# The first pair's scores as one float32 product of 66 rows

## The chip, the cores and the metric

The kernel runs on one core of a Trainium2 chip. The metric is the device time of one execution, in microseconds (us); lower is better. Each version's time is a median of several executions. A profiled execution has a time of its own; its span runs from the first to the last recorded instruction of the core.

In the rows, PE is TensorE's matmuls and PEld its weight loads, DVE is VectorE, ACT is ScalarE, POOL is GpSimd, and SP is the queue from which all this kernel's DMAs are issued, in order.

## The reference, cut to what matters

A causal attention with a decay bias feeds two feed-forward blocks. There are 4 batches of 8 heads, 576 positions and head size 64; the model width is 512.

```python
# attention, per head
scores = (q @ k.T) / sqrt(64)
cum    = cumsum(max(s, 0))
bias   = -(cum[q] - cum[k])                 # one number a position
scores = where(causal, -1e9, scores + min(bias, 0))
attn   = softmax(scores);  out = attn @ v
# block 1: gelu(x @ w_in) -> u, v; layer norm of v; u * (w_sg @ v_n + b_sg); x + (...) @ w_out
# block 2: mixes x with its shifted self by mu_k, mu_r; relu(xk @ w_k)**2 @ w_v * sigmoid(xr @ w_r)
```

## The kernel before, in words

Heads go through `attn_pair` in pairs, 16 pairs in all: pair 0 holds heads 0 and 1, pair 1 heads 2 and 3, and so on. The first four pairs, those of batch 0, come before any feed-forward work; later pairs are interleaved with `moe1`. While pairs 0 to 3 run, a generator called `prologue` converts the weights of block 1 from their 64-bit words: seven conversions (`sraw0` to `sraw6`). Conversion 0 to 3 fill `wv`, 4 to 6 fill `wcs`.

**Scores before.** A product of full accuracy is made of two fast ones. For each head the kernel loads keys and queries into one tile `kq` (keys in rows 0 to 63, queries in rows 64 to 127). ACT, DVE or POOL then cast them to the fast type fp32r (`qb`, `ka`), the rest that the cast loses is taken by two subtractions (`split_lo`), two DMAs copy the casts to the other half of the partitions (`qa`, `ka`), and two more put the running sums `cum`, split in the same way into `crt`, into rows of `QB` and `KB`. Each score chunk is then two matmuls of 128 rows: L252 with `qa`, `ka` and L253 with `qb`, `kb`.

**What follows a score chunk.** DVE adds the mask, takes the row minimum and writes `st` (L277). ACT takes the exponential (L285). PE transposes (`tp`), ACT or DVE copies the transposes to `pt`, and PE multiplies with the values (`pv`, L338, plain float32). Score chunks take turns in two PSUM banks, so PE may be at most two chunks ahead of DVE. A pair has nine steps: four of its first head, one that holds the last 64 rows of both heads, four of its second head. Its score chunks are of 128, 256, 384 and 512 columns for each head, and 512, 512, 64 and 64 for the common step: 3,712 columns.

**Buffers.** `kq` has two buffers, so a head's load has to wait until the casts and subtractions of the head two places earlier are done. A weight conversion takes three instructions on ACT (L76, L81, L87) and three on DVE (L82, L84, L69).

**What sets the order.** Each engine and the SP queue execute strictly in order. The order is set by a scheduler when the program is built; `PRO` says after how much of the attention each step of `prologue` is offered to it, and `after(late, early)` puts one instruction behind another in that order, without a wait. At most eight DMAs are in flight: DMA number i waits for number i - 8.

Of the kernel before, what the change touches and what calls it, by code (L numbers as in the profile page):

```python
# [8 lines left out]
F32 = mybir.dt.float32  # L9
# [28 lines left out]
def fused_kernel(ctx, tc, kqT, vL, s, w_in, g_ln, w_sgT, b_sg, w_out, mu_k, mu_r, w_k, w_v, w_r, out):  # L38
# [18 lines left out]
    def constants():  # L57
        after(nc.sync.dma_start(out=g_sb, in_=g_ln), last_row[0])
        nc.sync.dma_start(out=bsg, in_=b_sg.partition_broadcast(P))
        nc.sync.dma_start(out=mu[:, 0, 0], in_=mu_k)  # L60
        nc.sync.dma_start(out=mu[:, 1, 0], in_=mu_r)
        nc.vector.tensor_scalar(out=mu[:, :, 1], in0=mu[:, :, 0], scalar1=-1.0, scalar2=1.0, op0=ALU.mult, op1=ALU.add)
# [44 lines left out]
    qaf, kaf = (ep.tile([P, S], F32R, tag="u", name=n, bufs=4) for n in ("qa_f", "ka_f"))  # L107
    sums = [at.tile([P, 9], F32, tag=f"sums{i}", name=f"sums{i}", bufs=1) for i in range(2)]
# [7 lines left out]
    with tc.high_priority():  # L116
# [16 lines left out]
    make_identity(nc, ident)  # L133
    nc.gpsimd.memset(mhalf, -0.5)
    nc.gpsimd.memset(mask, 0.0)
    nc.gpsimd.affine_select(
        out=mask[:, 512:], in_=mask[:, 512:], pattern=[[-1, P]], compare_op=ALU.is_ge,
        fill=-BIG, base=0, channel_multiplier=1,
    )
# [65 lines left out]
    last_row = [None]  # L205


    def attn_pair(b, hp):
# [3 lines left out]
        for hh in range(2):  # L212
            h = 2 * hp + hh
            hd = b * H + h

            kq = at.tile([P, S], F32, tag="kq", name=f"kq{hd}", bufs=2)
# [645 lines left out]
```

## Time and profile before

| | |
|---|---|
| median of 3 executions | 679.77 us (679.13 to 683.0) |
| the profiled execution | 679.44 us |
| its span | 677.7 us; 1.74 us lie outside it |
| PE busy | 645.2 us, 95% of the span |
| DVE, ACT, POOL busy | 479.1, 416.0 and 219.7 us |
| DMA | 112.74 MB, mean 166 GB/s |

The busy shares are means over stages with different limits. The profile's 40 slices of 16.9 us show PE below 90% busy in its first five slices (3, 8, 6, 9, 9 tenths) and again around the eighth; from there on it is full to the end. [...]

### The profile page before, as it was taken

Reading aid. Unit: us, or ns where it says so; the run is one execution under the profiler, and the core shown is the slowest. Engines: PE = TensorE matmul, PEld = TensorE weight load, DVE = VectorE, ACT = ScalarE, POOL = GpSimd, SP = SyncE. Lnnn points to the kernel's source line nnn. Section 1 sums busy time; section 2 is a strip of 40 time slices with the busy share of each in tenths; the row PEclk is TensorE's granted clock in tenths of the full one; section 3 lists DMA queues with packets and bytes.
Section 4 is the critical chain, followed back from the end, with each engine's and each line's share of the span. In section 5 each row is a group of like instructions: output and inputs, shape, how many; then the busy total and the mean of one; then the engine's idle time right before and its main releaser. Section 6 shows DMA issues by size and latency. Waiting matters only on the chain.

```text
span 677.7 us, 11532 instructions
## 1 busy us (share of the span) xinstructions
PE 645.2 (95%) x3912; PEld 553.5 (82%) x3912; DVE 479.1 (71%) x995; ACT 416.0 (61%) x940; POOL 219.7 (32%) x233
## 2 busy tenths in 40 slices
PE   3869999799999999999999999999999999999997
PEld 2547676779878988877988899988888988999997
DVE  7876679986668645469644388787875959677863
ACT  5878777785558656368653285587755779543530
POOL 8556646368436459237363030000000000000000
PEclk9969999999999999999999999999999999999999
DMA  7764652455453532733510675567744593546643
GB/s 227 221 205 140 186 167 73 138 158 158 152 186 102 143 115 55 240 117 90 163 37 15 214 268 183 164 224 222 255 164 163 188 361 136 168 182 195 225 139 117
DMA packets 56459, 112.74 MB, mean 166 GB/s; under 512 B 7680, under 2 KB 20624, under 8 KB 56400
## 3 DMA queue, kind: packets, MB, share of 16 engines
q1 hardware_dynamic: 56400, 112.01, 52.3%
q8 instruction: 31, 0.51, 0.3%
q14 instruction: 28, 0.23, 0.1%
HBM read 74.46 MB, written 28.02 MB: 151 GB/s over the span
## 4 chain that ended last, share of the span: by engine, by line
PE 83%; DVE 6%; DMA 6%; ACT 2%; SPq 1%; issue 1%; POOL 0%; DVEq 0%; ACTq 0%; POOLq 0%
PE k L368 15%; PE sg L368 9%; PE pv L338 8%; PE r L368 7%; PE o L368 7%; PE psa L771 7%; PE u L368 6%; PE v L368 5%; PE tp L303 5%; PE psb L771 4%; PE sc L252 4%; PE sc L253 3%; PE psc L771 2%; DMA kq<-in_kqT_dram 1%; DMA wc<-wscr 1%
## 5 line engine op out<-in xcount | busy, mean ns | idle before, releaser
L368 PE MATMUL k<-x,wk 128*128 128x512 f32 (+1 forms) x480 | 101.4, 372 | 0.0
L368 PEld LDWEIGHTS k<-x,wk 128*128 128x128 f32 x480 | 83.6, 188 | 17.4
L252 PE MATMUL sc<-ka,qa 128*128 128x512 f32 (+3 forms) x180 | 64.0, 366 | 21.6 <-DVE mx L277 10.8
L285 ACT ACTIVATE st<-st,mx 128x128 f32<-128x128 f32 (+4 forms) x124 | 72.0, 582 | 19.3 <-DVE mx L277 18.8
L277 DVE CUSTOM_DVE_ANT_0 st<-sc,mask 128x512 f32<-128x512 f32 (+3 forms) x124 | 61.1, 503 | 27.7 <-PE sc L253 24.4
L368 PE MATMUL sg<-wsg,vn 128*128 128x288 f32 x448 | 65.2, 298 | 0.9 <-DVE u L502 0.9
L338 PE MATMUL pv<-pt,vf 128*64 128x320 f32 (+4 forms) x448 | 64.8, 366 | 0.2 <-ACT pt L305 0.2
L368 PEld LDWEIGHTS sg<-wsg,vn 128*128 128x128 f32 x448 | 60.8, 188 | 1.5 <-DVE u L502 1.1
L252 PEld LDWEIGHTS sc<-ka,qa 128*128 128x128 f32 x180 | 33.9, 189 | 32.1 <-DVE mx L277 15.1
L253 PE MATMUL sc<-KB,QB 128*128 128x512 f32 (+3 forms) x180 | 57.4, 335 | 1.0 <-DVE wv L69 1.0
L338 PEld LDWEIGHTS pv<-pt,vf 128*64 128x64 f32 x448 | 35.5, 137 | 23.5 <-issue 5.2
L303 PE MATMUL tp<-ident,st 128*128 128x128 f32 x300 | 49.5, 282 | 1.2 <-ACT st L285 1.0
L368 PE MATMUL r<-x,wr 128*128 128x512 f32 (+1 forms) x240 | 50.6, 372 | 0.0
L368 PEld LDWEIGHTS r<-x,wr 128*128 128x128 f32 x240 | 41.7, 188 | 8.8
L368 PE MATMUL v<-wv,xs 128*128 128x512 f32 x192 | 48.5, 397 | 0.0
L69 POOL TENSOR_TENSOR qa<-kq,QB 64x576 fp32r<-64x576 f32 x29 | 45.1, 1555 | 3.1 <-POOL st_f L283 1.0
L229 POOL CAST QB<-kq 64x576 fp32r<-64x576 f32 x28 | 21.1, 757 | 73.6 <-PE sc L253 44.3
L69 POOL TENSOR_TENSOR KB<-kq,ka 64x576 fp32r<-64x576 f32 x29 | 43.5, 1499 | 3.9 <-ACT ka L230 1.9
L303 PEld LDWEIGHTS tp<-ident,st 128*128 128x128 f32 x300 | 35.6, 142 | 10.6 <-ACT st L285 4.6
L368 PE MATMUL o<-gh,wc 128*128 128x288 f32 x192 | 40.8, 298 | 0.8 <-DMA wc<-wscr 0.8
L368 PEld LDWEIGHTS v<-wv,xs 128*128 128x128 f32 x192 | 35.1, 188 | 7.5 <-POOL QB L229 0.5
L368 PE MATMUL u<-xs,wc 128*128 128x288 f32 x288 | 40.9, 297 | 0.0
(188 smaller groups left out, 1451.8 us busy)
## 6 DMA issues: line engine op xcount, KB each, us to landing
wc<-wscr SPq DMA_DIRECT2D x24, 512.0 KB
kq<-in_kqT_dram SPq DMA_DIRECT2D x32, 288.0 KB
kr<-kdram SPq DMA_DIRECT2D x12, 768.0 KB
kdram<-k SPq DMA_DIRECT2D x16, 512.0 KB
yt<-ydram SPq DMA_DIRECT2D x24, 257.0 KB
vf<-in_vL_dram SPq DMA_DIRECT2D x16, 320.0 KB
ydram<-y SPq DMA_DIRECT2D x16, 288.5 KB
gt<-gdram SPq DMA_DIRECT2D x12, 384.0 KB
```

Source lines behind the costliest of these rows:

```text
L69: eng.tensor_tensor(out=lo, in0=x, in1=f32(hi), op=ALU.subtract)
L229: (nc.scalar.copy if hd < 2 else nc.gpsimd.tensor_copy)(qb[64:128], kq[64:128])
L252: nc.tensor.matmul(sc[:m, :c1 - c0], qa[:, q], ka[:, c0:c1], start=True, stop=False)
L253: nc.tensor.matmul(sc[:m, :c1 - c0], qb[:, q], kb[:, c0:c1], start=False, stop=True)
L277: mi = nc.vector.tensor_tensor_reduce(out=st[:, c0:c1], in0=sc[:, :n], in1=mk, op0=ALU.add, op1=ALU.min, scale=-SCALE, scalar=mx[:, 0:1] i ...
L285: e = nc.scalar.activation(st[:, :w], st[:, :w], AF.Exp, bias=mx[:, last:last + 1], scale=-1.0, accum_out=sm[:, i + 5 * (hh == 1):i + 5 * ...
L303: nc.tensor.transpose(tp[:, c:c + P], st[:, j * P:(j + 1) * P], ident)
L338: nc.tensor.matmul(acc[64 * a:64 * a + 64, o:n], vf[:, a, kk], pt, start=(kk == 0), stop=(kk == nk - 1))
L368: nc.tensor.matmul(acc, a, w_, start=(i == 0), stop=(i == n - 1))
L771: nc.tensor.matmul(ps[:, c, :HW], l, r, start=(start and i == 0), stop=(i == len(mms) - 1), skip_group_check=True)
```

## The change

The change is in the first microseconds and in the order of the DMAs behind them. It does six things.

1. Heads 0 and 1 no longer use `kq`, the casts, the subtractions and the copies. Queries go straight into rows 0 to 63 of a float32 tile `QF`, keys into rows 0 to 63 of `KF`. Row 64 of `QF` holds `cum` and row 64 of `KF` holds -1; row 65 of `QF` holds 1 and row 65 of `KF` holds `cum`. One plain float32 matmul over these 66 rows gives score and bias together.
2. `cum` goes to those rows directly, as an unsplit float32 row, by four small DMAs.
3. The casts of heads 2 and 3 move to ACT (they stood on POOL and DVE), and those of heads 0 and 1 are gone.
4. The raw weights' first two loads are put behind those four rows (`first_rows`), and so are the values' load of pair 0; the four loads of `constants` (`g_sb`, `bsg`, two of `mu`) all stand behind the last sums issued so far, where before only the first did.
5. The sets of `QB` and `KB` are filled in another order, those of `QB` on DVE.
6. `PRO` offers the first conversion at once, the second and third after pair 0, and the others closer together.

```diff
     def constants():
-        after(nc.sync.dma_start(out=g_sb, in_=g_ln), last_row[0])
-        nc.sync.dma_start(out=bsg, in_=b_sg.partition_broadcast(P))
-        nc.sync.dma_start(out=mu[:, 0, 0], in_=mu_k)
-        nc.sync.dma_start(out=mu[:, 1, 0], in_=mu_r)
+        for i in (nc.sync.dma_start(out=g_sb, in_=g_ln),
+                  nc.sync.dma_start(out=bsg, in_=b_sg.partition_broadcast(P)),
+                  nc.sync.dma_start(out=mu[:, 0, 0], in_=mu_k),
+                  nc.sync.dma_start(out=mu[:, 1, 0], in_=mu_r)):
+            after(i, last_row[0])
...
+    QF = [ep.tile([P, S], F32, tag="xT", name=f"QF{i}", bufs=8) for i in range(2)]
+    KF = [ep.tile([P, S], F32, tag="xT", name=f"KF{i}", bufs=8) for i in range(2)]
...
-        for i in range(NSET + 1):
-            eng = nc.gpsimd if i else nc.vector
-            eng.memset(f32(QB[i][0:64]), 1.0)
-            eng.memset(f32(KB[i][0:64]), 0.0)
-            eng.memset(f32(KB[i][0:4]), -1.0)
+        for i in range(2):
+            nc.vector.memset(QF[i][64:66], 1.0)
+            nc.gpsimd.memset(KF[i][64:66], -1.0)
...
+    for i in range(NSET + 1):
+        nc.vector.memset(f32(QB[i][0:64]), 1.0)
+        nc.gpsimd.memset(f32(KB[i][0:64]), 0.0)
+        nc.gpsimd.memset(f32(KB[i][0:4]), -1.0)
...
-                if i == 0:
-
-                    after(d, last_row[0])
+                if i < 2:
+                    after(d, first_rows[0])
...
+            if pr < 1:
+                qf, kf = QF[hh], KF[hh]
+                nc.sync.dma_start(out=qf[0:64], in_=kqT[b, h][64:128])
+                nc.sync.dma_start(out=kf[0:64], in_=kqT[b, h][0:64])
+                nc.sync.dma_start(out=qf[64:65], in_=cum[hd:hd + 1])
+                last_row[0] = nc.sync.dma_start(out=kf[65:66], in_=cum[hd:hd + 1])
+                ops.append((qf, kf))
+                if hh == 0:
+                    vf, x_t, load_v = outputs(b, hp, pr, h)
+                elif hd == 1:
+                    after(load_v, last_row[0])
+                    first_rows[0] = last_row[0]
+                yield 0
+                continue
...
-            (nc.scalar.copy if hd < 2 else nc.gpsimd.tensor_copy)(qb[64:128], kq[64:128])
-            (nc.vector.tensor_copy if 1 < hd < H else nc.scalar.copy)(ka[0:64], kq[0:64])
+            (nc.scalar.copy if hd < 4 else nc.gpsimd.tensor_copy)(qb[64:128], kq[64:128])
+            (nc.vector.tensor_copy if 3 < hd < H else nc.scalar.copy)(ka[0:64], kq[0:64])
...
-            lo = nc.vector if hd == 0 else nc.gpsimd
-            split_lo(lo, qa[64:128], kq[64:128], qb[64:128])
-            split_lo(lo, kb[64:128], kq[0:64], ka[0:64])
+            split_lo(nc.gpsimd, qa[64:128], kq[64:128], qb[64:128])
+            split_lo(nc.gpsimd, kb[64:128], kq[0:64], ka[0:64])
...
         def scores(sc, hh, q, c0, c1, m):
+            if len(ops[hh]) == 2:
+                qf, kf = ops[hh]
+                nc.tensor.matmul(sc[:m, :c1 - c0], qf[0:66, q], kf[0:66, c0:c1], start=True, stop=True)
+                return
             qa, ka, qb, kb = ops[hh]
...
-    PRO = [0, 0] + [1 + 0.75 * i for i in range(5)]
+    PRO = [1e-6, 2.05, 2.05, 2.3, 2.6, 3.25, 4]
```

The first place is DVE's start. Here `scr` holds the sums (the TENSOR_SCALAR clips them, and the scan that stands as SCALAR_TENSOR_TENSOR adds them up), and `crt` their split. Before:

```order
L122 MEMSET scr_97 32x576
L126 MEMSET QB0_84 64x576
L127 MEMSET KB0_86 64x576
L129 TENSOR_SCALAR scr_97<-scr_97 32x576
L128 MEMSET KB0_86 4x576
L130 SCALAR_TENSOR_TENSOR scr_97<-scr_97 32x576
L69 TENSOR_TENSOR qa0_130<-kq0_126,QB0_84 64x576
L69 TENSOR_TENSOR KB0_86<-kq0_126,ka0_131 64x576
L69 TENSOR_TENSOR crt_98<-scr_97,crt_98 32x576
```

DVE's start in the changed kernel:

```order
L125 MEMSET scr_101 32x576
L127 MEMSET QF0_92 2x576
L127 MEMSET QF1_93 2x576
L140 MEMSET QB0_84 64x576
L140 MEMSET QB1_85 64x576
L140 MEMSET QB_f_88 64x576
L135 TENSOR_SCALAR scr_101<-scr_101 32x576
L136 SCALAR_TENSOR_TENSOR scr_101<-scr_101 32x576
L70 TENSOR_TENSOR crt_102<-scr_101,crt_102 32x576
L301 ISA st_f0_147,mx0_0_0_148<-sc0_0_0_0_149,mask_83 128x128
```

Six memsets now stand ahead of the TENSOR_SCALAR where three did, the one between it and the scan is gone, and the two subtractions of head 0 are gone too.

The second place is the SP queue where the loads of heads 4 and 5 (`kq4`, `kq5`) stand. Before, they come behind the copies of heads 3 and 4, and `kq5` behind the reciprocals of pair 0 (`rdram`):

```order
L217 DMA kq4_528<-in_kqT_dram 128x576
L222 DMA QB1_85<-crt_98 2x1x576
L223 DMA KB1_87<-crt_98 2x1x576
L232 DMA ka3_349<-ka3_349 64x576
L231 DMA qa3_348<-QB0_84 64x576
L232 DMA ka4_533<-ka4_533 64x576
L188 DMA sraw4_415<-in_w_in_dram 128x4x256 x2
L231 DMA qa4_532<-QB1_85 64x576
L321 DMA rdram_65<-rc0_298 9x128
L217 DMA kq5_543<-in_kqT_dram 128x576
```

In the changed kernel they stand behind the second raw weight (`sraw0` here names the tile that weights 0 and 1 share) and the constants, the 23rd to 33rd DMA:

```order
L163 DMA sraw0_153<-in_w_in_dram 128x1024
L160 DMA cumd_62<-crt_102 32x1152
L58 DMA g_sb_67<-in_g_ln_dram 128x4
L59 DMA bsg_68<-in_b_sg_dram 128x576
L60 DMA mu_69<-in_mu_k_dram 128x4
L61 DMA mu_69<-in_mu_r_dram 128x4
L241 DMA kq4_508<-in_kqT_dram 128x576
L246 DMA QB1_85<-crt_102 2x1x576
L247 DMA KB1_87<-crt_102 2x1x576
L241 DMA kq5_523<-in_kqT_dram 128x576
L163 DMA sraw2_329<-in_w_in_dram 128x1024 x2
```

So `kq5` has moved ahead of the third and fourth raw weight and of `rdram`, while the constants have moved back to just before `kq4`.

The third place is DVE behind pair 0's common step, in the changed kernel. `syt0` is a weight in conversion, `mu` the small instruction on the two `mu` loads, `ka4` the cast of head 4:

```order
L70 TENSOR_TENSOR wv_98<-syt0_154,wv_98 128x512
L301 ISA st_f0_147,mx0_2_4_193<-sc0_2_4_0_194,mask_83 128x512
L301 ISA mx0_2_4_193 128x1
L301 ISA st_f0_147,mx0_2_4_193<-sc0_2_4_1_198,mask2_131,mx0_2_4_193 128x64
L301 ISA mx0_2_4_193 128x1
L63 TENSOR_SCALAR mu_69<-mu_69 128x2x4
L83 SCALAR_TENSOR_TENSOR syt0_154<-sraw0_153,syt0_154 128x512
L301 ISA st0_1_0_214,mx0_1_0_215<-sc0_1_0_0_216,mask_83 128x128
L301 ISA mx0_1_0_215 128x1
L254 CAST ka4_513<-kq4_508 64x576
```

Before, the instruction on `mu` stood ahead of DVE's first score chunk, both of these conversions were through before the second head's first chunk, and no cast of head 4 stood here.

## Rows read from the trace of the kernel before

**Rows 1.** Busy time in four stretches (us, then busy us and count per engine, PEclk).

```profile
12.65:45.99 33.34, 24.58 (x125) 17.52 (x125) 26.60 (x65) 26.27 (x69) 18.11 (x16) 0.87 0.64 187
...
45.99:78.60 32.61, 31.17 (x211) 21.94 (x211) 20.78 (x65) 28.73 (x82) 23.25 (x20) 0.98 0.58 173
...
37.35:47.59 10.24, 8.07 (x30) 6.22 (x32) 9.06 (x26) 7.30 (x21) 5.32 (x5) 0.50 0.67 201
...
100.00:130.00 30.00, 26.40 (x169) 20.55 (x167) 28.77 (x62) 21.26 (x55) 16.96 (x19) 1.00 0.35 100
...
130.00:170.00 40.00, 37.52 (x264) 33.31 (x265) 31.50 (x84) 28.93 (x81) 26.33 (x23) 0.96 0.51 155
```

**Rows 2.** Chain that ended last, 0 to 45 us: start us, us, what.

```profile
1.18 3.05 DMA kq<-in_kqT_dram
...
8.65 0.61 SPq L223
...
9.30 5.17 DMA sraw<-in_w_in_dram
...
18.05 6.04 DMA kq<-in_kqT_dram
...
30.19 4.33 DMA rdram<-rc
```

**Rows 3.** ACT in order of time; in brackets its idle time before, and what ended it.

```profile
12.65 0.40 ACT L285 ACTIVATE st_f<-st_f,mx 128x128 f32<-128x128 f32 x1 [2.60 <-DVE mx L277]
...
37.77 0.78 ACT L285 ACTIVATE st_f<-st_f,mx 128x576 f32<-128x576 f32 x1 [1.90 <-DVE mx L277]
...
40.12 0.65 ACT L313 COPY pt<-tp 128x256 f32<-128x256 f32 x2 [1.09 <-PE tp L303]
...
41.87 0.62 ACT L87 CAST wcs<-syt 128x512 fp32r<-128x512 f32 x1 [1.10 <-DVE syt L84]
...
45.99 0.39 ACT L285 ACTIVATE st_f<-st_f,mx 128x128 f32<-128x128 f32 x1
...
99.18 0.68 ACT L200 CAST wsg<-wsr 128x576 fp32r<-128x576 f32 x1 [1.29 <-DMA wsr<-in_w_sgT_dram]
```

**Rows 4.** DVE in order of time, at the start and around 36 us.

```profile
2.63 0.70 DVE L129 TENSOR_SCALAR scr<-scr 32x576 f32<-32x576 f32 x1
...
3.86 1.28 DVE L130 TENSOR_TENSOR_SCAN scr<-scr 32x576 f32<-32x576 f32 x1
...
12.25 0.29 DVE L277 CUSTOM_DVE_ANT_0 st_f<-sc,mask 128x128 f32<-128x128 f32 x1 [0.61 <-PE sc L253]
...
35.97 0.97 DVE L230 CAST ka_f<-kq 64x576 fp32r<-64x576 f32 x1 [2.14 <-DMA kq<-in_kqT_dram]
```

**Rows 5.** The SP queue in order of time, around 30 us.

```profile
30.59 0.36 SPq L217 DMA_DIRECT2D kq<-in_kqT_dram  x1
```

**Rows 6.** Chain that ended last, 88 to 100 us.

```profile
91.92 1.44 DMA rdram<-rc
```

**Rows 7.** The values' tile, 20 to 35 us (pair 0): count, ns min/median/max, forms.

```profile
L338 PE MATMUL pv<-pt,vf x28: 219/404/483, 26.8 to 31.4; 128*64 128x320 f32 x12, 128*64 128x256 f32 x4, 128*64 128x128 f32 x4, 128*64 128x192 f32 x4
```

**Rows 8.** PE by shape, 45 to 80 us: count | busy us, mean ns | idle.

```profile
L338 PE MATMUL pv<-pt,vf 128*64 128x320 f32 x36 | 7.6, 441 | 0.0
...
L338 PE MATMUL pv<-pt,vf 128*64 128x64 f32 x12 | 1.7, 220 | 0.0
...
L253 PE MATMUL sc<-KB_f,QB_f 128*128 128x512 f32 x2 | 0.8, 390 | 0.0
...
L253 PE MATMUL sc<-KB_f,QB_f 128*128 128x256 f32 x1 | 0.3, 279 | 0.0
```

**Rows 9.** PE in order of time: two score products of 512 columns.

```profile
14.05 0.63 PE L253 MATMUL sc<-KB,QB 128*128 128x512 f32 x1
...
42.82 0.63 PE L253 MATMUL sc<-KB,QB 128*128 128x512 f32 x1
```

More of the change, by code (lines that the diff above doesn't have):

```diff
@@ L122, in fused_kernel @@
         nc.vector.memset(one, 1.0)
-        for i in range(NSET + 1):
-            eng = nc.gpsimd if i else nc.vector
-            eng.memset(f32(QB[i][0:64]), 1.0)
-            eng.memset(f32(KB[i][0:64]), 0.0)
-            eng.memset(f32(KB[i][0:4]), -1.0)
+        for i in range(2):
+            nc.vector.memset(QF[i][64:66], 1.0)
+            nc.gpsimd.memset(KF[i][64:66], -1.0)
+        make_identity(nc, ident)
+        nc.gpsimd.memset(mask, 0.0)
+        nc.gpsimd.affine_select(
+            out=mask[:, 512:], in_=mask[:, 512:], pattern=[[-1, P]], compare_op=ALU.is_ge,
+            fill=-BIG, base=0, channel_multiplier=1,
+        )
         nc.vector.tensor_scalar(out=s_sb, in0=s_sb, scalar1=0.0, scalar2=8.0, op0=ALU.max, op1=ALU.mult)
@@ L132, in fused_kernel @@
         split_lo(nc.vector, cr[:, 1], cum, cr[:, 0])
-    make_identity(nc, ident)
+    for i in range(NSET + 1):
+        nc.vector.memset(f32(QB[i][0:64]), 1.0)
+        nc.gpsimd.memset(f32(KB[i][0:64]), 0.0)
+        nc.gpsimd.memset(f32(KB[i][0:4]), -1.0)
     nc.gpsimd.memset(mhalf, -0.5)
[L135 to L139, printed above, removed]
     mask2 = at.tile([P, 64], F32, tag="mask2", name="mask2", bufs=1)
@@ L203, in fused_kernel, with outputs @@
     xT = {}
-    last_row = [None]
+    last_row, first_rows = [None], [None]
+    def outputs(b, hp, pr, h):
+        vf = at.tile([P, 2, NT, D], F32, tag="vf", name=f"vf{pr}", bufs=2)
+        load_v = nc.sync.dma_start(out=vf, in_=vL[b][:, h:h + 2])
+        x_t = ep.tile([P, S], F32, tag="xT", name=f"xT{pr}", bufs=8)
+        xT[(b, hp)] = x_t
+        return vf, x_t, load_v
     def attn_pair(b, hp):
@@ L228, in attn_pair @@
                 qa, ka = qaf, kaf
-            (nc.scalar.copy if hd < 2 else nc.gpsimd.tensor_copy)(qb[64:128], kq[64:128])
-            (nc.vector.tensor_copy if 1 < hd < H else nc.scalar.copy)(ka[0:64], kq[0:64])
+            (nc.scalar.copy if hd < 4 else nc.gpsimd.tensor_copy)(qb[64:128], kq[64:128])
+            (nc.vector.tensor_copy if 3 < hd < H else nc.scalar.copy)(ka[0:64], kq[0:64])
             nc.sync.dma_start(out=f32(qa[0:64]), in_=f32(qb[64:128]))
             nc.sync.dma_start(out=f32(ka[64:128]), in_=f32(ka[0:64]))
-            lo = nc.vector if hd == 0 else nc.gpsimd
-            split_lo(lo, qa[64:128], kq[64:128], qb[64:128])
-            split_lo(lo, kb[64:128], kq[0:64], ka[0:64])
+            split_lo(nc.gpsimd, qa[64:128], kq[64:128], qb[64:128])
+            split_lo(nc.gpsimd, kb[64:128], kq[0:64], ka[0:64])
             ops.append((qa, ka, qb, kb))
             if hh == 0:
-                vf = at.tile([P, 2, NT, D], F32, tag="vf", name=f"vf{pr}", bufs=2)
-                nc.sync.dma_start(out=vf, in_=vL[b][:, h:h + 2])
-                x_t = ep.tile([P, S], F32, tag="xT", name=f"xT{pr}", bufs=8)
-                xT[(b, hp)] = x_t
+                vf, x_t, load_v = outputs(b, hp, pr, h)
             yield 0
```

## The prediction, on record before the changed kernel ran

> **What bounds the kernel now.** I read the table of stages first, then the chain of work that ended last, then each engine in order of time around the places where the chain names a DMA. The page has PE nearly full from its sixth slice on, so a microsecond saved ahead of that point should be a microsecond at the end; what has to be found is what paces the first 80 us. PE does not. Between the first exponential, at 12.65, and the first exponential of pair 2, at 45.99, ACT works 26.27 us of 33.34, DVE 26.60 and PE 24.58; from there to 78.60, about where the feed-forward products begin, ACT works 28.73 of 32.61 and DVE only 20.78 [rows 1]. ACT is the engine with the least to spare over the whole start, so I keep the account on ACT: a gain has to come out of its idle time, 33.34 - 26.27 = 7.07 us up to pair 2.
>
> The chain shows where that idle time is from: a weight that takes 5.17 us to land, a head's load that takes 6.04, and the reciprocals' trip through DRAM at 30.19, 4.33 us [rows 2]. On ACT three waits stand together, 1.90, 1.09 and 1.10 us at 37.77, 40.12 and 41.87 [rows 3], and they have one source: DVE is in order and waits 2.14 us for head 5's keys and queries at 35.97 [rows 4], because SP issued that load only at 30.59 [rows 5], behind head 4's copies and the reciprocals. Everything behind that cast stands still: the common step's reduction, its exponential, PE's transposes. [...]
>
> **The change, part by part.**
>
> *The start.* A first reduction needs sums in place. The clipping of the sums starts at 2.63 and the scan at 3.86; between them are 1.23 us, of which 0.70 are the clipping and 0.53 the one memset there [rows 4]. Three more memsets now stand ahead (+1.6) and the one between is gone (-0.53), so the scan ends 1.1 us later, at 3.86 + 1.28 + 1.1 = 6.2. In exchange no split of the sums, no cast and no subtraction comes before the rows. SP then issues the sums' rows at 0.61 each [rows 2]: the second, the last that head 0 needs, at 6.9. What such a row takes alone no row shows. The bounds are 1.44 us, the reciprocals' 4.5 KB at 91.92 [rows 6], and 4.33, the same transfer with raw weights in the queue [rows 2]. Only 1.2 MB were issued before, by 4 us, and 288 KB as the first load took 3.05 [rows 2], so the queue should be empty; I take 2.2, near the lower end. First product at 9.1.
>
> [...]
>
> With the 4.33 us of the loaded queue it would come 2.1 later.
>
> *The products.* The values' product is the only plain float32 product in the trace. Pair 0 has 14 of them in the code (two by two, five by two) and 28 records [rows 7]: two records each. From 64 to 320 columns a record grows by 441 - 220 ns over 256 columns, 0.86 ns a column; an fp32r record grows from 279 to 390 over 256, 0.43 [rows 8]. So a float32 product costs 1.7 ns a column against 0.87 for the two fp32r products. Over 3,712 columns that is 6.4 us in place of 3.2, at the upper clock. The clock is low at first: a 512-column product at 14.05 takes 0.63, as at 42.82 where 0.50 is granted, against 0.39 [rows 9, 8]. So 3.4 ns a column at first. First chunk: 0.44, plus about 0.25 to DVE (the constant part of a record, 390 ns less 512 columns of 0.43 ns, is 0.17; the rest is my estimate of the hand-over), reduction at 9.8 instead of 12.25 [rows 4]; exponential at 10.3 instead of 12.65. The next two chunks pace ACT: 256 and 384 columns take 0.87 and 1.31 where the exponentials before them take about 0.5 and 0.6, so ACT waits 1.1 us that it did not wait before. Bounds: 0.2 if the clock is up at once, 2.5 if the 512-column chunk (1.74) is waited for too; behind it stand conversion 0's two ACT instructions, which cover it if their weight has landed.
>
> *What lies behind.* Before 12.65, ACT had conversion 0 behind it; now that lies after. A conversion is three ACT instructions like the cast at 41.87, 0.62 to 0.75 each less their overlap, 1.8 us. So the start is 2.35 earlier with 1.8 more to do; alone it gains 0.5. Casts for the first four heads are the same number on ACT up to there.
>
> *The loads.* The second raw weight is the 23rd DMA: counted from 6.2 at 0.61 for the small ones, about 0.4 for the large, issued near 15.1 instead of 9.30. Landing takes 3.05 to 5.17 [rows 2]: 18.2 to 20.3. The two `mu` loads follow at 17.4; DVE reaches the `mu` instruction, behind pair 0's common step, at about 19.3, and the second head's first reduction is queued behind it, with its exponential and transposes behind that. By the same two durations `mu` is there at 19.4 to 21.4 (behind the weight), and conversion 1 is late together with it. I take 1.2 us of ACT idle; bounds 0 and 2.5. Head 4's load is issued near 18 and head 5's near 19.4, eleven microseconds ahead of 30.59. Even at 6.04 it is there at 25.4, and its cast, 54th on DVE, is due after 30. So the three waits of 4.09 us go, and with them the stretch at 0.50.
>
> *The account.* From 10.3: work 26.27, plus conversion 0 (1.8), less what is still owed when pair 2's first exponential comes (the last casts of conversions 4 and 5, and one copy: 1.7), is 26.4. Idle 7.07 - 4.09 + 1.1 + 1.2 = 5.3. Pair 2 starts at 42.0 instead of 45.99: 4.0 earlier. The 1.7 owed are paid in the next stretch, so 2.3 stay. DVE owes some 3 us there as well (most of conversions 4 and 5), hidden in its 11.8 us of idle time [rows 1]; were it not, the gain would be gone.
>
> *Later.* In the new order the last piece of `w_sg` is issued ahead of the reciprocals' three broadcasts instead of behind them; ACT waits 1.29 us for it at 99.18 [rows 3]. But DVE is busy 28.77 of 30 us from 100 to 130 [rows 1], and waits for those broadcasts too. I count half, 0.6. Everything else behind 78.60 keeps its work and, but for neighbours, its order.
>
> Sum: 679.44 - 2.3 - 0.6 = **676.5 us** for an execution like the profiled one, which is 0.33 below the median; against the median it is -0.5%.
>
> **The rivals.**
>
> *More: the waits go and no new one comes.* The rows land early, the clock rises soon since PE has no gaps, `mu` is there. Then the 1.1 and 1.2 are not paid: 674.2. And the short fall of the clock after 130 (mean 0.96 over 40 us, so 3.4 us at half speed [rows 1]) may not come back: up to 1.7 more, 672.5. Against it: the second weight is surely issued six microseconds later than before.
>
> *Nothing: the loads are only moved.* Rows with 4.33 instead of 2.2 (2.1 late) and `mu` and weight 1 at the upper bound (1.3 more than taken) eat 3 of the 2.9: 679.5 to 680. For it: the queue before shows 5 and 6 us as often as 3 [rows 2].
>
> *Slower: PE is the bound at its lower level.* [...] If the clock stayed at 0.50 until pair 2, PE's 24.58 us of work in the stretch of rows 1 (a part at half speed already) plus 3.2, at half speed throughout, would be over 40, from 9.1 to 50 at least, in place of 42.0: 676.5 + 8 = 684.5. It decides once some 13 us of PE's work that ACT waits for run at half speed in place of full (6.5 us: the gain and 0.5% more). Against it: before, PE came up to full level after 7 us with gaps, and float32 leaves it fewer. [...]
>
> **How the numbers follow.** A measurement here tells about 0.5%, 3.4 us, from no change. The forecast's own range, by the bounds 0.2 to 2.5, 0 to 2.5 and 0 to 1.3, is 674 to 679; the line of 0.5% (676.4) runs through it: 0.62, of which 0.28 faster and 0.34 same. More: 0.14, faster. Nothing: 0.10, nearly all same, 0.03 beyond it on the slow side. Slower: 0.14. That makes faster 0.42, same 0.41, slower 0.17. The range that leaves out 2 in 10 reaches from the far end of the first rival to past "nothing": 672.5 to 681.5.
>
> **What would show it.** Right: the scan ends near 6.2; DVE's first reduction comes near 9.8; no DVE wait for head 5's keys; PE at 1.00 through 37 to 47; pair 2's first exponential at 42; feed-forward products 2 to 3 us ahead of 78.6. Each step wrong: the first reduction after 11 (the rows are slow), DVE idle over 2 us before `mu`, or ACT idle over 2 us in front of conversion 1. The whole is wrong if pair 2 comes 4 us early and the end does not: then DVE between 100 and 130, or the reciprocals' trips there, have taken it back.

## The result, and the profile after

The changed kernel is slower. Its median is 686.1 us (685.95 to 687.23, 4 executions) against 681.13 for the kernel before on the same chip (679.13 to 683.0, 4 executions): a ratio of 1.0076, with a 95% interval of 1.0047 to 1.0105. 676.5 was predicted, and the time lies above the predicted range.

The profiled execution took 686.12 us with a span of 684.3. The page's line of busy times for the changed kernel:

```profile
PE 654.8 (96%) x3912; PEld 556.8 (81%) x3912; DVE 476.7 (70%) x993; ACT 415.0 (61%) x940; POOL 213.4 (31%) x231
```

PE was busy 645.2 us of 677.7 before. Its busy time has grown by 9.6 us and its idle time has shrunk by 3.0 (684.3 - 654.8 = 29.5 against 32.5): together the 6.6 us of the span. So over the whole span PE did not wait more: its work took longer. Most of that lies at the start, where PE is busy 65.24 us up to 83.70, against 57.34 up to 78.60 before. Busy time in stretches of the changed kernel, with the columns of [rows 1]:

```profile
9.49:31.37 21.88, 21.36 (x54) 11.86 (x55) 11.47 (x36) 14.12 (x36) 8.88 (x9) 1.00 0.82 225
12.65:45.99 33.34, 28.57 (x121) 17.42 (x119) 21.52 (x60) 25.35 (x64) 15.77 (x14) 0.99 0.71 194
45.99:78.60 32.61, 28.48 (x170) 20.67 (x172) 21.84 (x63) 26.24 (x76) 15.37 (x13) 0.86 0.57 168
45.02:51.85 6.83, 5.63 (x21) 3.56 (x22) 6.38 (x14) 5.68 (x16) 0.19 (x1) 0.50 0.76 227
62.09:65.50 3.41, 3.41 (x12) 2.82 (x13) 2.18 (x8) 2.88 (x10) 1.21 (x1) 0.50 0.24 70
```

The first row is the stretch of pair 0: PE is busy for 21.36 of 21.88 us, ACT for only 14.12. The column PEclk, the granted share of PE's clock, says 1.00 there, but the trace's record of the clock begins only with its first change, a rise at 31.37, and what stands ahead of it is written as 1.00. The durations show the level. PE of the changed kernel in order of time:

```profile
30.86 0.63 PE L277 MATMUL sc<-KB_f,QB_f 128*128 128x512 f32 x1
31.28 0.44 PE L276 MATMUL sc<-ka,qa 128*128 128x512 f32 x1
31.56 0.40 PE L277 MATMUL sc<-KB,QB 128*128 128x512 f32 x1
...
46.22 0.80 PE L276 MATMUL sc<-ka,qa 128*128 128x512 f32 x1 [3.27 <-DVE mx L301]
...
61.96 0.49 PE L276 MATMUL sc<-ka,qa 128*128 128x256 f32 x1 [2.47 <-DVE mx L301]
```

A 512-column product takes 0.63 up to 31.37 and 0.40 from there, the two durations that stood for the two levels in [rows 8, 9]. All score products of pair 0 ended by 27.80, at the lower level. The last two rows are new gaps on PE, 3.27 and 2.47 us, both in front of a chunk that waits for DVE; the clock falls in or right behind them (the last two stretches of the table above). DVE in order of time:

```profile
5.53 1.35 DVE L136 TENSOR_TENSOR_SCAN scr<-scr 32x576 f32<-32x576 f32 x1
...
10.82 0.29 DVE L301 CUSTOM_DVE_ANT_0 st_f<-sc,mask 128x128 f32<-128x128 f32 x1 [2.46 <-DMA KF<-scr]
...
23.09 0.17 DVE L63 TENSOR_SCALAR mu<-mu 128x8 f32<-128x8 f32 x1 [2.32 <-DMA mu<-in_mu_r_dram]
...
34.40 0.93 DVE L344 RECIPROCAL rc<-rc 9x128 f32<-9x128 f32 x1
...
44.55 1.27 DVE L376 TENSOR_TENSOR xT<-xT,rb 128x576 f32<-128x576 f32 x1 [2.31 <-DMA rb<-rdram]
...
59.15 1.95 DVE L376 TENSOR_TENSOR xT<-xT,rb 128x576 f32<-128x576 f32 x1
```

The first reduction comes 1.43 us earlier than in [rows 4], and no instruction waits for head 5's keys. By the trace this reduction waits for a sums' row (`KF<-scr`), the fourth, head 1's, which landed at 10.55; its own product had ended at 10.26. In the code its output `st_f` has the one buffer of the tile `scr`, from which all four rows are copied. Behind that DVE waits for `mu`, and at 44.55 it waits 2.31 us for `rb`, the reciprocals of pair 0 back from DRAM, with pair 2's second reduction queued behind. That multiplication (L376) of pair 0 and the one of pair 1 at 59.15 stand ahead of PE's two gaps. ACT in order of time:

```profile
11.21 0.40 ACT L309 ACTIVATE st_f<-st_f,mx 128x128 f32<-128x128 f32 x1 [0.85 <-DVE mx L301]
...
19.65 0.48 ACT L331 COPY pt<-tp 128x384 f32<-128x384 f32 x1 [2.14 <-PE tp L327]
...
21.00 0.67 ACT L77 ACTIVATE syt<-sraw 128x512 f32<-128x512 f32 x1 [0.87 <-DMA sraw<-in_w_in_dram]
...
31.36 0.39 ACT L309 ACTIVATE st_f<-st_f,mx 128x128 f32<-128x128 f32 x1
...
43.11 0.66 ACT L77 ACTIVATE syt<-sraw 128x512 f32<-128x512 f32 x1 [1.54 <-DMA sraw<-in_w_in_dram]
...
45.99 0.39 ACT L309 ACTIVATE st_f<-st_f,mx 128x128 f32<-128x128 f32 x1
```

In the kernel before, pair 1's first exponential and pair 0's reciprocal stand here (all engines in order of time):

```profile
25.96 0.39 ACT L285 ACTIVATE st_f<-st_f,mx 128x128 f32<-128x128 f32 x1
...
29.22 0.94 DVE L320 RECIPROCAL rc<-rc 9x128 f32<-9x128 f32 x1
```

The first exponential is 1.44 us earlier, pair 1's comes at 31.36 in place of 25.96, 5.4 later, and pair 2's at 45.99 in both kernels. The middle stretch won back what the first lost (no stretch at 0.50 from 37 to 45), and then the two gaps came: pair 3's first exponential is 3.2 late (62.80 for 59.62), pair 4's 5.1 (77.10 for 71.99).

### The profile page after: what moved, and what is told of

It is laid out like the page before. It is cut to its first block, busy times and chain, and to the rows that moved or that the text cites. A ratio compares the mean times of both kernels' runs of the same rounds, so it can differ in the third digit from the quotient of the medians.

```text
span 684.3 us, 11525 instructions
## 1 busy us (share of the span) xinstructions
PE 654.8 (96%) x3912; PEld 556.8 (81%) x3912; DVE 476.7 (70%) x993; ACT 415.0 (61%) x940; POOL 213.4 (31%) x231
## 4 chain that ended last, share of the span: by engine, by line
PE 76%; DVE 9%; DMA 7%; ACT 3%; issue 2%; SPq 2%; POOL 0%; DVEq 0%; ACTq 0%; POOLq 0%
PE k L392 15%; PE sg L392 7%; PE r L392 7%; PE pv L362 7%; PE o L392 7%; PE psa L795 7%; PE u L392 5%; PE tp L327 4%; PE v L392 4%; PE psb L795 4%; PE sc L276 3%; PE sc L277 3%; DMA rb<-rdram 2%; PE psc L795 2%; DVE st L301 1%
## 5 line engine op out<-in xcount | busy, mean ns | idle before, releaser
L276 PE MATMUL sc<-ka,qa 128*128 128x512 f32 (+3 forms) x168 | 58.5, 357 | 10.9 <-DVE mx L301 9.9
L362 PE MATMUL pv<-pt,vf 128*64 128x320 f32 (+4 forms) x448 | 66.5, 371 | 0.6 <-DVE pt L331 0.5
L277 PE MATMUL sc<-KB,QB 128*128 128x512 f32 (+3 forms) x168 | 52.9, 330 | 0.0
L276 PEld LDWEIGHTS sc<-ka,qa 128*128 128x128 f32 x168 | 31.1, 185 | 20.7 <-DVE mx L301 13.7
L70 POOL TENSOR_TENSOR KB<-kq,ka 64x576 fp32r<-64x576 f32 x28 | 41.2, 1471 | 7.9 <-ACT ka L254 5.9
L70 POOL TENSOR_TENSOR qa<-kq,QB 64x576 fp32r<-64x576 f32 x28 | 42.2, 1507 | 2.1
L253 POOL CAST QB<-kq 64x576 fp32r<-64x576 f32 x27 | 19.6, 728 | 68.9 <-PE sc L277 51.8
```

Source lines behind the costliest of these rows:

```text
L70: eng.tensor_tensor(out=lo, in0=x, in1=f32(hi), op=ALU.subtract)
L253: (nc.scalar.copy if hd < 4 else nc.gpsimd.tensor_copy)(qb[64:128], kq[64:128])
L276: nc.tensor.matmul(sc[:m, :c1 - c0], qa[:, q], ka[:, c0:c1], start=True, stop=False)
L277: nc.tensor.matmul(sc[:m, :c1 - c0], qb[:, q], kb[:, c0:c1], start=False, stop=True)
L362: nc.tensor.matmul(acc[64 * a:64 * a + 64, o:n], vf[:, a, kk], pt, start=(kk == 0), stop=(kk == nk - 1))
```

## The experiments

Three explanations stand against each other. **Products**: the float32 products make PE pace pair 0. **Loads**: weight 1 and `mu`, issued behind everything, and the waits that follow from them. **Order**: the new `PRO` and the place of the constants. In the kernels marked "order held" each engine and the SP queue keep the changed kernel's order, by ordering edges without waits, so that only the named edit differs; the scheduler would otherwise reorder. What an edit adds stands outside that order, and the bookkeeping for it is left out of the code below. The expectations have much the same three under the names PACE (later CLOCK), CONSTANTS (later LOADS) and ORDER. Rows with - and + below are instructions in the order of one engine.

**Cheaper products** (`one_fast_pass`, order held): the same 66 rows in one pass of the upper halves, as bfloat16.

```diff
-    nc.tensor.matmul(sc[:m, :c1 - c0], qf[0:66, q], kf[0:66, c0:c1], start=True, stop=True)
+    qh, kh = (x[0:66].bitcast(BF16).rearrange("p (n two) -> p n two", two=2)[:, :, 1] for x in (qf, kf))
+    nc.tensor.matmul(sc[:m, :c1 - c0], qh[:, q], kh[:, c0:c1], start=True, stop=True)
```

> The order on every engine is held as in the changed kernel; the first pair's score products read only the upper 16 bits of each float32 (one bfloat16 pass), so these scores lose their low part. Theory PACE (the float32 products at the low clock set the pace of the start, and all that comes later follows from that): the clock rises near 17 to 20 us instead of 31.4, pair 1's first exponential comes at 25 to 27 instead of 31.4, pair 0's reciprocals are back before DVE asks for them, PE's idle time of 3.3 us at 43 goes, and the end is 6 to 10 us ahead of the changed kernel, 0 to 4 ahead of the kernel before. Theory ORDER (the multiplication's place and the queue's new order cost it, whatever the products take): DVE still waits about 2 us for the reciprocals in pair 2, and the gain on the changed kernel is under 3. Theory CONSTANTS (weight 1 and mu, issued late, hold DVE): pair 1's first exponential stays within 2 us of 31.4.

Measured: 685.79 against 681.05, ratio 1.007 (1.0043 to 1.0097). PE is no longer the bound in pair 0 (first row below, busy times), yet pair 1's first exponential comes at 30.37, only 1.0 us earlier:

```profile
9.50:30.57 21.07, 12.71 (x41) 7.25 (x41) 11.45 (x37) 13.86 (x35) 8.77 (x9) 1.00 0.83 232
```

What took the place of the products, on DVE:

```profile
22.88 0.17 DVE L332 TENSOR_SCALAR mu<-mu 128x8 f32<-128x8 f32 x1 [4.08 <-DMA mu<-in_mu_r_dram]
```

and on ACT:

```profile
20.23 0.66 ACT L346 ACTIVATE syt<-sraw 128x512 f32<-128x512 f32 x1 [2.86 <-DMA sraw<-in_w_in_dram]
```

Making the products cheap gains about nothing by itself, as CONSTANTS expected: the wait for `mu`, 2.32 us in the changed kernel, grows to 4.08 and that for weight 1 from 0.87 to 2.86. Two things pace pair 0 side by side.

**Earlier loads** (`early_loads`, order held; `early_fast` has the products of `one_fast_pass` too), on SP:

```diff
 DMA kq<-in_kqT_dram x2
+DMA mu<-in_mu_k_dram
+DMA mu<-in_mu_r_dram
+DMA bsg<-in_b_sg_dram
 DMA QF<-scr
...
 DMA vf<-in_vL_dram
-DMA sraw<-in_w_in_dram
+DMA sraw<-in_w_in_dram x2
```

> The changed kernel, order held, but for four loads on SP: the two of mu and bsg are issued ahead of the first pair's rows (SP is idle there), and raw weight 1 right behind raw weight 0. Theory LOADS (mu and weight 1, issued 10 and 7 us later than in the kernel before, hold DVE and ACT in order; with the float32 products alone replaced pair 1's first exponential came only 1.0 earlier): DVE's wait for mu of 2.3 us goes, weight 1 lands by 15 instead of 21, but the float32 products are then what is waited for, pair 1's first exponential at 29 to 30.5 instead of 31.4. Theory PACE (the products alone): as in the changed kernel, within 0.5. End: 0 to 2 us earlier for either.

> Both at once: the four loads early, and the first pair's products in one bfloat16 pass (their low part is left out). If the start has two limits side by side, products and loads, of which each alone hides the other (TWO LIMITS): pair 1's first exponential at 23 to 26, 5 to 8 us ahead of the changed kernel, where each edit alone gives 1 to 2; the end 3 to 6 earlier, if the later order lets it through. If a third thing bounds the start: still 29 or more.

Measured: 686.46 against 680.8, 1.0078 (1.0051 to 1.0104), and 684.74, 1.0049 (1.0023 to 1.0074). With the loads alone pair 1 starts at 29.63 and pair 2 at 43.80, 2.2 us earlier than 45.99; the end does not move. The edit has a price of its own: behind these loads head 0's second row, issued at 7.06, holds the first product until 10.44, where in the changed kernel 7.63 and 9.49 stand. The clock rises at 24.12 here, still within pair 0. PE of `early_loads` has the same two gaps, each 1.7 to 2.8 us earlier:

```profile
44.48 0.71 PE L543 MATMUL sc<-ka,qa 128*128 128x512 f32 x1 [3.27 <-DVE mx L568]
...
59.20 0.58 PE L543 MATMUL sc<-ka,qa 128*128 128x256 f32 x1 [2.48 <-DVE mx L568]
```

With both edits pair 1 starts at 28.18, still 2.2 later than before, and pair 2 at 43.98. A third wait shows there: DVE stands 2.14 us for head 4's load, up to 21.83.

**The multiplications** (`mult_later`: pair 0's alone; `mults_later`: pair 1's too, and with it the cast of its rows on ACT and their split on POOL; order held). DVE, pair 0's:

```diff
-TENSOR_TENSOR xT<-xT,rb
 ISA st_f,mx_1<-sc_1,mask 128x256
...
 RECIPROCAL rc<-rc
+TENSOR_TENSOR xT<-xT,rb
 ISA st_f,mx_4<-sc_4,mask 128x512
```

> The changed kernel with its order held on every engine but for one row: on DVE, pair 0's multiplication by the reciprocals stands behind pair 1's reciprocal instead of behind pair 2's first reduction. PACE: pair 1's first exponential stays at 31.4, the wait of 2.3 us is gone, but most of the loss is older: the end comes 0 to 2 us earlier. ORDER: DVE's wait of 2.3 and PE's idle time of 3.3 at 43 go, the clock doesn't fall at 45 (6.8 us at half level cost 3.4), pair 3's first exponential comes at 58 to 60 instead of 62.8, and the end 4 to 5 us earlier. CONSTANTS: no change over 1 us.

> The changed kernel, order held, but for the multiplications by the reciprocals of pair 0 and pair 1: both one place later (pair 0's behind pair 1's reciprocal, pair 1's behind pair 3's fourth reduction, with its cast on ACT and its subtraction on POOL). Moving pair 0's alone brought 1.5 us by pair 3 and nothing at the end. ORDER: the idle time of PE of 2.5 us at 59.5 goes, and the clock's fall at 62 (3.4 us at half level), pair 4's first exponential at 73 to 74.5 instead of 77.1; the end 2 to 4 us earlier. If the later stages take it back: pair 4 early, the end within 1 us of the changed kernel.

Measured: 686.25 against 681.05, 1.0066 (1.0043 to 1.009), and 685.86 against 680.8, 1.0068 (1.0041 to 1.0095). In `mult_later` the gap of 3.27 is gone (1.10 is left), and the clock falls all the same at 44.16. Ahead of that fall, from 40.75, PE was busy for 1.64 of 3.41 us; behind it, at 0.50, it is nearly full:

```profile
44.16:50.99 6.83, 6.10 (x21) 3.47 (x22) 6.16 (x11) 5.90 (x18) 1.05 (x1) 0.50 0.91 273
```

In `mults_later` both gaps are gone and the clock stays up to 63.18. Pair 3 starts at 59.95 instead of 62.80, and then PE meets the next wait:

```profile
63.73 0.76 PE L544 MATMUL sc<-ka,qa 128*128 128x512 f32 x1 [3.45 <-DMA ka<-ka]
```

Its chain of work shows what that was:

```profile
57.48 0.72 SPq L523
...
58.26 5.34 DMA ka<-ka
```

Head 7's two copies were issued at 57.48 and 58.26, behind the reciprocals' broadcasts, a weight and a pair's values, and took 5.34 us. Pair 4 starts at 77.23, as in the changed kernel.

**The rows** (`rows_128`, order held): the same product over 128 rows, of which 62 hold ones times zeros.

```diff
-    nc.vector.memset(QF[i][64:66], 1.0)
+    nc.vector.memset(QF[i][64:128], 1.0)
+    nc.gpsimd.memset(KF[i][64:128], 0.0)
...
-    nc.tensor.matmul(sc[:m, :c1 - c0], qf[0:66, q], kf[0:66, c0:c1], start=True, stop=True)
+    nc.tensor.matmul(sc[:m, :c1 - c0], qf[:, q], kf[:, c0:c1], start=True, stop=True)
```

> The changed kernel, order held, with the first pair's float32 products over all 128 rows, the 62 added rows being ones times zeros. A product takes as long as before by its columns. If the rows in use decide the clock, it rises by 20 us instead of 31.4, pair 1's first exponential comes at 26 to 28, and the end is 3 to 6 us earlier. If it is the float32 product as such that leaves the clock low, it rises near 31 again, and the time is within 1.5 us of the changed kernel's.

Measured: 684.59 against 681.05, 1.0048 (1.0023 to 1.0072). The record of the clock has its first rise at 15.82 in place of 31.37; its stretches, as in the table above:

```profile
9.50:15.82 6.32, 6.25 (x13) 3.11 (x13) 2.37 (x9) 4.20 (x12) 4.92 (x5) 1.00 0.79 225
15.82:22.65 6.83, 4.17 (x19) 1.98 (x17) 2.52 (x7) 3.50 (x7) 0.00 (x0) 1.00 0.85 228
22.65:26.07 3.42, 3.12 (x9) 1.91 (x10) 2.88 (x10) 2.35 (x9) 1.93 (x2) 0.50 0.62 184
```

Its 512-column products in the second stretch (PE by shape: count | busy us, mean ns):

```profile
L542 PE MATMUL sc<-KF,QF 128*128 128x512 f32 x2 | 1.5, 829 | 0.0
...
L542 PE MATMUL sc<-KF,QF 128*64 128x512 f32 x2 | 1.1, 618 | 0.0
```

and in the changed kernel from 15.9 to 31:

```profile
L273 PE MATMUL sc<-KF,QF 66*128 66x512 f32 x4 | 3.9, 1079 | 0.0
```

With 66 rows a record of 512 columns takes 1.08 us throughout in the changed kernel; with 128 rows it takes 0.83 and 0.62 once the clock is up. Before the rise the two are alike (0.63 for 256 columns in both). Yet pair 1 starts only at 30.71: PE's work is through sooner, and the loads hold pair 0 (DVE waits 3.96 us for `mu`, ACT 2.44 for weight 1).

**A warm clock** (`warm`, order held): 18 products of 128 rows ahead of the first score.

```diff
+    for i in range(18):
+        nc.tensor.matmul(spare, ones[:, :P], ones, start=True, stop=True)
```

> The changed kernel, order held, with 18 added fp32r products of 128 rows and 512 columns of ones into a bank that nobody reads, from about 1.5 us to the first score. If PE's clock only wants earlier work, it is up when the scores start, a float32 chunk of 512 columns takes 0.9 us instead of 1.9, pair 1's first exponential comes at 26 to 28, and the end 3 to 6 us earlier (PACE), under 1 earlier (ORDER). If float32 products don't keep it up, it falls again within the first pair, and the gain is under 2.

Measured: 687.32 against 681.05, 1.0087 (1.0056 to 1.0117). The clock rose at 5.11 and fell at 11.94, 2.5 us after the first product of 66 rows. PE also had gaps of 1.93 and 0.82 us in between, so the fall alone does not tell the products from the gaps:

```profile
5.11:11.94 6.83, 4.08 (x17) 2.58 (x17) 3.04 (x7) 4.14 (x8) 6.64 (x10) 1.00 0.48 136
11.94:32.42 20.48, 19.43 (x51) 10.70 (x50) 11.61 (x35) 13.68 (x35) 6.70 (x7) 0.50 0.82 228
```

With a recorded 0.50 PE is then busy 19.43 of 20.48 us. So it is not only a late rise from a cold start: here the clock had been up, and it stayed down through pair 0 with PE nearly full.

**The kernel before, with head 5's load early** (`before_load`, order of before held, a third buffer for `kq`), on SP:

```diff
 DMA qa<-QB
+DMA kq<-in_kqT_dram
...
 DMA rdram<-rc
-DMA kq<-in_kqT_dram
```

> The kernel before, its order held, with a third buffer for keys and queries and head 5's load moved on SP from behind the reciprocals to behind head 3's copies (25 instead of 30.6 us). This is the prediction's term of the loads by itself: the three waits on ACT (4.1 us from 37.8 to 41.9) go and the clock doesn't fall at 37: pair 2's first exponential 3 to 5 us earlier, the end 2 to 4 us ahead of the kernel before. If the reciprocals or the conversions are what ends last there: 0 to 1.

Measured: 680.15 against 680.8, 0.9975 (0.9952 to 0.9998). Pair 2 starts at 44.21, 1.8 earlier, and pair 4 at 72.81, 0.8 later than before: ACT now waits 1.92 us for DVE in a weight's conversion, at 40.09, and there is again a stretch at 0.50, from 38.10 to 44.92. At pair 2 the prediction's main item brings 1.8 us of the 4.1 that were counted; at the end it is worth 1.7 us by itself (0.0025 of 681; 0.1 to 3.3 by the interval).

**The start and the order apart.** `start_alone` is the changed kernel with the old `PRO` (its first two entries 1e-6 in place of 0) and with only the first of the constants held back; `order_alone` is the kernel before with the new `PRO` and constants. `start_rows` and `start_fast` are `start_alone` with the edits of `rows_128` and `one_fast_pass`. The order is the scheduler's in the first two; the last two hold that of `start_alone`.

```diff
-    PRO = [1e-6, 2.05, 2.05, 2.3, 2.6, 3.25, 4]
+    PRO = [1e-6, 1e-6] + [1 + 0.75 * i for i in range(5)]
```

> The changed kernel without two of its parts: PRO offers the conversions as in the kernel before (the first two from pair 0's first step), and of the constants only g_sb is put behind the sums. The float32 products and the rows ahead of the raw weights stay. ORDER (the conversions and constants that now come later leave DVE and ACT work and waits between 40 and 80 us): PE's idle time of some 4 us between 46 and 78 goes, and the time is within 2 us of the kernel before. CLOCK (the first pair's float32 products leave PE at its lower level, and PE is short of time up to the end): the clock rises late again (after 25 us), and the time stays 3 to 6 us above the kernel before.

> The kernel before with the change's PRO and its place for the constants, and nothing else. ORDER: 3 to 6 us above the kernel before, with DVE waiting for mu and PE idle for 2 us and more between 40 and 65. CLOCK: within 2 us of the kernel before.

> As start_alone, its order held, with the float32 products over 128 rows (62 of ones times zeros). CLOCK: the clock rises by 18 us as it did with 128 rows in the changed kernel's order, some 8 us of PE's work are done at twice the rate, and the time is 2 to 4 us below start_alone. ORDER: under 1 below.

> As start_alone, its order held, with one bfloat16 pass for each float32 product of the first pair (their low part is left out). CLOCK and the products together bound the start: 3 to 6 us below start_alone, 1 to 4 below the kernel before. If another wait takes the products' place, as in the changed kernel's order: under 1.5 below start_alone.

Measured against 680.31: `start_alone` 685.34, 1.0074 (1.005 to 1.0099); `order_alone` 681.45, 1.0012 (0.9989 to 1.0035); `start_rows` 685.42, 1.0065 (1.0036 to 1.0095); `start_fast` 685.79, 1.007 (1.0048 to 1.0092). The order alone costs nothing that shows (by the interval, up to 2.4 us). The start alone costs as much as the whole change, but not in the same way: `start_alone` has nearly caught up by pair 4 (72.77 for 71.99); then DVE waits for pair 3's reciprocals:

```profile
81.53 0.76 DVE L375 TENSOR_TENSOR xT<-xT,rb 128x576 f32<-128x576 f32 x1 [5.81 <-DMA rb<-rdram]
```

In the changed kernel that multiplication, at 85.77, waits 0.28. So these two kernels do not divide the loss; they show that it comes without the new order too. In `start_rows` the clock is up at 15.66 and that wait takes 7.36 us: an early clock alone isn't enough.

**That multiplication, and the rows behind the weights.** `start_mult` puts pair 3's multiplication behind pair 4's common step on DVE. `weights_first`, `weights_first_fast` and `weights_first_rows` have that, and the first two raw weights ahead of the sums' rows on SP:

```diff
 DMA mu<-in_mu_r_dram
+DMA sraw<-in_w_in_dram x2
 DMA kq<-in_kqT_dram x2
...
 DMA vf<-in_vL_dram
-DMA sraw<-in_w_in_dram x2
```

> start_alone, its order held, but for pair 3's multiplication by its reciprocals, which stands behind pair 4's common step on DVE instead of ahead of it (its cast on ACT and the cast of xq with it). RECIPROCALS (DVE's wait of 5.8 us at 76 to 82 holds pair 4 and PE): pair 4's common step at 79 to 80 instead of 84.9, the end 2 to 4 us below start_alone. If PE has other work to do meanwhile: under 1.5.

> As start_mult, and the loads of raw weights 0 and 1 stand ahead of the first pair's rows on SP, as in the kernel before. WEIGHTS (their landing at 14 to 19 holds ACT, in whose order their conversions stand ahead of the pair's exponentials): ACT's waits for them of 4.3 us go, the rows land up to 2 us later, pair 1's first exponential at 29 to 31 instead of 33.0, and the end 1 to 3 us below start_mult. PRODUCTS (float32 at the low clock holds pair 0 anyway): pair 1's first exponential stays above 31.5, the end within 1 of start_mult.

> As weights_first, with one bfloat16 pass for each float32 product (their low part is left out). If reciprocals, weights and products together are what the change costs: pair 1's first exponential at 24 to 27, the end 3 us or more below weights_first and at or below the kernel before. If it stays 3 us or more above the kernel before, something else in the new start costs it.

> As weights_first, with the float32 products over 128 rows (62 of ones times zeros). If the clock rises by 17 (it did with 128 rows in two other orders), the products hold less: pair 1's first exponential 1 to 3 us ahead of weights_first, the end 1 to 3 us below it, at about the kernel before. If the clock's gain is taken back by PE's gaps, as it was in start_rows: within 1 of weights_first.

Measured against 681.17: 686.2, 1.008 (1.0053 to 1.0108); 689.91, 1.0124 (1.0081 to 1.0168); 688.91, 1.0107 (1.0056 to 1.0159); 689.48, 1.0121 (1.0075 to 1.0167). Without the wait on `rb`, PE of `start_mult` waits 2.08 us for a cast of the feed-forward input on ACT (`xs`), up to 87.27. In `weights_first` PE's first product starts at 14.10, not 9.80, and the first exponential at 15.46, not 11.10. So the change is right to put the rows ahead of the weights.

**All waits off, then the rows too** (order held). `waits_off` has the SP edit of `early_loads`, the edits of `mults_later`, and on SP the copies of head 7 and one of head 8 ahead of broadcasts. `waits_off_rows` has the rows of `rows_128` as well.

```diff
+DMA qa<-QB
+DMA ka<-ka
 DMA rb<-rdram x3
 DMA wscr<-wcs
 DMA vf<-in_vL_dram
-DMA qa<-QB
-DMA ka<-ka
```

> The changed kernel, order held, with the edits of early_loads and of mults_later together, and on SP the copies of head 7 (and one of head 8) ahead of the reciprocals' broadcasts instead of behind them. CHAIN (each wait removed alone let the next one through): PE's idle times of 3.3 us at 41 to 46 and of 2.5 to 3.5 at 57 to 64 go, pair 4's first exponential at 71 to 73 instead of 77.1, the end 3 to 6 us below the changed kernel, within 2 of the kernel before. If more holes of that size follow behind 64: under 2 below the changed kernel.

> As waits_off, with the float32 products over 128 rows (62 of ones times zeros). If the clock's late rise still costs something once the waits are gone (CLOCK): it rises by 17, pair 1's first exponential 1 to 3 us ahead of waits_off, the end 1 to 3 us below it. If another engine holds the start: within 1 of waits_off.

Measured, against the same 680.51: `waits_off` 683.51 (12 executions), 1.0042 (1.0023 to 1.0061); `waits_off_rows` 680.41 (12 executions), 0.9996 (0.9975 to 1.0018). From 38 to 75 us no gap of PE over 1.85 is left in `waits_off`. Its stretches:

```profile
9.40:29.84 20.44, 19.57 (x52) 11.35 (x52) 10.72 (x33) 13.01 (x33) 8.52 (x9) 1.00 0.81 227
...
43.49:50.32 6.83, 5.78 (x21) 3.32 (x22) 6.38 (x12) 6.22 (x19) 1.30 (x1) 0.50 0.93 263
```

and `waits_off_rows`:

```profile
9.40:14.66 5.26, 4.20 (x9) 2.44 (x10) 1.30 (x6) 2.64 (x9) 4.97 (x5) 1.00 0.78 237
14.66:41.97 27.31, 21.55 (x123) 13.30 (x121) 21.59 (x60) 23.89 (x62) 14.35 (x12) 1.00 0.74 200
```

The first rise of the clock is at 29.84 in the one (PE busy 19.57 of the 20.44 us ahead of it) and at 14.66 in the other. Ratios to the kernel before, with the first exponentials of pairs 1, 2 and 4:

| | 66 rows | 128 rows |
|---|---|---|
| the changed kernel's waits | 1.0076 (1.0047 to 1.0105): 31.36, 45.99, 77.10 | 1.0048 (1.0023 to 1.0072): 30.71, 44.90, 75.56 |
| waits off | 1.0042 (1.0023 to 1.0061): 30.43, 45.29, 73.08 | 0.9996 (0.9975 to 1.0018): 28.68, 42.52, 71.70 |

Between the two of the lower line, and between the two of the right column, the intervals do not meet; from the upper left corner each single step goes the same way, but there the intervals overlap. Together the two edits take back all that the change cost and no more: the kernel is level with the one before, whose pairs 1, 2 and 4 start at 25.96, 45.99 and 71.99. The starts are those of one profiled execution each, and that of `waits_off_rows` took 683.44, above its median of 680.41 (its granted clock was 0.989, and 0.993 in the execution of 680.48): the trace shows the earlier starts, the 12 executions the end.

## Why the prediction was wrong

*The start* held, with one wait left out. The scan ended at 6.88 (6.2 predicted); head 0's second row was issued at 7.63 (6.9), and the first product came 1.86 us later (2.2 was taken), at 9.49 (9.1). But the first reduction came at 10.82, not 9.8: it waited for all four rows, and the sum had counted the two that head 0's product needs. The first exponential was 1.44 earlier, not 2.35. The fourth row, 2.3 KB from SP, took 1.68 us (issued at 8.87, landed at 10.55).

*The products* failed, by size. The cost of 3.4 ns a column at the lower level was right (on the chain of work a 512-column product of two records, at 26.02, takes 1.78 us; 1.74 by the prediction), but the step let the clock rise soon and charged 1.1 us of ACT's waiting. The clock stayed low until pair 1, ACT waited 2.14 us for PE at 19.65 and 1.11 at 28.26, and 66 rows instead of 128 are worth 3.1 us at the end once the other waits are gone (683.51 - 680.41, on one chip). The rival *Slower* had this mechanism, PE as the bound at its lower level. But it was rated low because float32 leaves PE no gaps; no run shows that a fuller PE brings the rise sooner (21.36 of 21.88 us were busy ahead of the one at 31.37). It also priced that mechanism alone at 8 us; `one_fast_pass` shows that taking PE's bound away alone gains nothing here, since the loads were as late. That its 684.5 lies near 686.1 is in part luck: it had the clock low until pair 2, while it rose as pair 1 began, and it had none of the waits behind.

*The loads* failed too. The three waits around 40 us in [rows 3] did go, and so did the clock's stretch at 0.50 behind them (37.35 to 47.59 in [rows 1]). Weight 1 landed at 21.0 and `mu` at 23.1, outside the 18.2 to 20.3 and 19.4 to 21.4, and `early_loads` shows them worth 2.2 us at pair 2. Only when PE has room does their price show in full: 4.08 us on DVE.

*The account* failed in what stood behind it. It held that a gain up to pair 2 stays at the end but for conversions that are owed. Pair 0 ended late, so its reciprocal came at 34.40 in place of 29.22, the reciprocals' broadcasts were issued at 39.22 to 40.40 and landed at 44.5, with pair 2's second reduction behind them on DVE, which is in order. *The account* had looked at DVE's idle total from 46 to 78 and called what DVE owes hidden; the trace shows two gaps of PE, up to 46.22 and up to 61.96, and the experiments peeled them one by one: `early_loads`, `mult_later` and `mults_later` each remove a wait, and none moves the end clear of the noise. Off all together they give 0.0034 of the ratio, 2.3 us (overlapping intervals), and with 128 rows 0.0052, 3.5 us (intervals that do not meet). And the gain was priced too high: `before_load` puts head 5's early load at 1.8 us at pair 2, where the three waits had been counted at 4.09.

*Later*: ACT's wait for the piece of `w_sg` fell from 1.29 us to 0.63 (at 102.17); what that is worth at the end was not tested by itself.

What stays open: why the clock fell at 44.16 in `mult_later` and not in `mults_later`, whose order is the same up to there; how the rest of the loss divides between the loads and pair 0's products, which hide one another; and whether the edits of `waits_off`, none of which was tried on the kernel before, would make that kernel faster too. If they would, a part of what they give back is not the change's loss.

## What to carry to other kernels

A step that removes one long wait should be priced by the next wait of its size, read engine by engine for the pair behind it; where everything is in order, removing waits one at a time may show nothing until the last is gone. Before PE's idle time is filled with dearer products, see at which clock level they will run, and test that with a form of the same product. A test of one cause alone can show zero for each of two causes that pace the same stretch: take both away before dropping either.

## What the hardware showed that was not expected

PE's clock stayed at its lower level while float32 products of 66 rows, with pair 0's transposes between them, filled PE (21.36 us busy of 21.88 in the changed kernel, 19.43 of 20.48 at 0.50 in `warm`). With 128 rows its first rise came at 15.82 (`rows_128`), 15.66 (`start_rows`) and 14.66 (`waits_off_rows`), with 66 float32 rows and no products ahead at 31.37 in the changed kernel and 29.84 in `waits_off`. The rows are not all of it: in `early_loads`, with 66, it rose at 24.12, amid pair 0's products. In these runs busy time by itself did not lift it, and the number of rows in use did change it (15.82 in `rows_128` for 31.37, with PE busy 6.25 of the 6.32 us ahead of that rise). What decides it they do not show. Products of one pass with the same 66 rows rose late as well (30.57 in `one_fast_pass`), but there PE was busy only 12.71 of 21.07.

The multiplications by `rb`, 0.68 to 0.76 us in `mults_later`, took 1.27 and 1.95 in the changed kernel. POOL there, in order of time:

```profile
43.81 1.40 POOL L70 TENSOR_TENSOR qa<-kq,QB 64x576 fp32r<-64x576 f32 x1
...
58.96 1.52 POOL L70 TENSOR_TENSOR xs<-xT,xs 128x576 fp32r<-128x576 f32 x1
```

POOL's instructions end at 45.21 and 60.48, and DVE's end 0.61 and 0.62 us later (45.82 and 61.10), a little less than the 0.68 that such a multiplication takes at its shortest. Two runs bear on it with the order held: in `mult_later` pair 0's multiplication, at 49.64, stood in a stretch without a POOL instruction (45.21 to 52.07) and took 0.68; in `early_loads` pair 1's, at 56.38, began 0.18 behind POOL's split, as here, and took 1.95 again. What ties the two ends together was not shown.
